# A fused recurrence and ELU feed-forward kernel on one core: a new order of vector work around three places, four closing additions on GpSimd, and the last two pairs' products interleaved

## The chip, the cores and the metric

One Trainium2 chip; the program runs on 1 of its cores. The metric is device time in microseconds (us), the median of several runs. Engines are named as in the profile: PE (TensorE, with PEld for its weight loads), DVE (VectorE), ACT (ScalarE), POOL (GpSimd), SP (SyncE, which issues most DMAs).

## The reference

```python
# q, k, v, f_logit: (4, 8, 768, 48) float32
f = 1.0 / (1.0 + np.exp(-f_logit))
for t in range(S):                       # S = 768
    state = f[:, :, t, :, None] * state + np.einsum('bhd,bhe->bhde', k[:, :, t], v[:, :, t])
    y[:, :, t] = np.einsum('bhd,bhde->bhe', q[:, :, t], state)
x = y.transpose(0, 2, 1, 3).reshape(3072, 384)
h = x @ w_in                             # w_in: (384, 2048)
g = np.where(h > 0.0, h, np.exp(np.minimum(h, 0.0)) - 1.0)
out = g @ w_out                          # w_out: (2048, 384)
```

## The kernel before, in words

The 3072 tokens are cut into 12 units of 256 tokens (`NU`), numbered 0 to 11, three to a batch. Each unit goes through the recurrence in chunked form ("attention") and then through the two matrix products of the feed-forward block. The hidden width 2048 is 16 blocks of 128, taken as 8 pairs per unit (index `P`, `m` the unit, `j` the pair). Everything is float32, and TensorE takes each float32 product in two passes, so a product counts as x2 in the profile.

**Up-products.** Units 0 and 1 compute `x @ w_in` directly (`up`, L980). From unit 2 on, `phase` (L954) computes four 128x128 blocks of hidden (a "quad", two pairs) with fewer products: a fast matrix scheme with 20 products of 128x128 per quad, in five phases of 3, 5, 5, 4 and 3 products. It uses precombined weights (`w_sums`, on DVE and POOL) and precombined inputs (`blend`, L938, six ops on POOL). Quad n has two PSUM banks, side 0 and side 1, under the tags h0 and h1; the side that quad n holds first is the tag that quad n+1 takes second. ACT copies the results of phases 0, 1 and 2 into the buffer `vals` (L968), and after phase 1 writes one of them back into the bank as the start of a sum (the "seed", L970), which phase 3 then adds to. DVE finishes the quad with `joins` (L946, L952): `JOIN3` and `JOIN4` read PSUM banks (3 and 2 instructions), `MID` and `LAST` read only `vals` (2 and 1 instructions). A bank is free for the next quad when the joins that read it are done.

**ELU.** `exped` (L972) runs two ACT instructions per pair, relu and exp, after `LAST`. `elu` (L993) runs one DVE instruction per pair (L996, tile `gg`), and then four POOL instructions (L1006, tile `sums`) that combine the four 128x128 blocks of `gg`.

**Down-products.** `down` (L1010) computes `g @ w_out` with seven products of 192 columns per pair (again a fast scheme), into four PSUM banks psM 0 to 3 of the unit (tags m0 to m3). Three products take `gg`, four take `sums`. After a unit's last pair (j = 7) its closing additions follow (L1061 to L1079): a copy of bank 0's first half to `u2`, then DVE additions that read the banks into the output tile `o`, and four stores on SP.

**Attention.** `attention` (L900) places per unit: `decays` (L696: a DVE scan, a DVE reciprocal, and POOL multiplications of k and q by the factors), three per unit, and `settle`; `transposed`; `both` (L891: `advance` on PE into psU under tags a0 and a1, `scores` on PE into the tags m3 and m0, `mask` on DVE, L773, and four state steps on DVE, L746); `outputs` (L794, PE, psY under tags a0 and a1 again); and `carried`.

**Order.** The order on each engine is the order in which the Python code issues it (a manual schedule). From unit 2 on, the loop at L1286 goes through 100 steps s; a step does two phases, the joins, the elus that are due, the attention work planned for this time (`at_step`, time T = 32 + 2s; a unit's time base is `base(u)`, 20 per unit), and some of the down-products from a running stream (`take`, which counts products). So each engine works its own queue in order, and waits at its head for what it needs. Steps 3 and 4 (131 to 139 us) hold three things at once: unit 1's last products and its closing additions, unit 2's second quad, and unit 3's `both`.

## Time and profile before

| what | value |
|---|---|
| median of 3 runs | 549.93 us (549.87, 549.93, 552.82) |
| the profiled execution: its own time | 551.41 us |
| its span, first to last instruction | 549.7 us |
| mean granted TensorE clock | 0.996 |
| PE busy | 531.6 us (97%) |
| DVE, ACT, POOL busy | 406.0, 313.6, 330.3 us |

A row of a timeline reads: start in us, length in us, engine, line, operation, output<-inputs, shape, count, and in brackets the engine's idle time ahead of it with what ended it. A row with x2 or more holds several instructions that followed each other. Matmuls are pipelined, so a PE row's length reaches beyond the start of the next one; start times are the better measure.

### The profile page before, as it was taken

The page shows a single profiled execution, that of the slowest core. Times are in us where ns is not written, and L with a number is a line of the kernel's source. Part 1 is how long each engine was busy: PE and PEld are TensorE (multiplying, and loading weights), DVE is VectorE, ACT ScalarE, POOL GpSimd, SP SyncE. Part 2 cuts the span into 40 slices and gives each one's busy share as a digit, 9 for nine tenths or more (in the row PEclk, how much of TensorE's full clock was granted, in tenths as well). Part 3 has the DMA queues.
Part 4 walks back from the last instruction along what each step waited for, and adds up shares of the span by engine and source line. Part 5 has one row for each costly group of instructions (what it writes and reads, how often), then busy time and mean ns, then how long its engine had stood idle before and what let it go on. Part 6 is the DMA issues. An engine that isn't in the chain of part 4 may idle for free.

```text
span 549.7 us, 15601 instructions
## 1 busy us (share of the span) xinstructions
PE 531.6 (97%) x6294; PEld 494.1 (90%) x6294; DVE 406.0 (74%) x721; ACT 313.6 (57%) x643; POOL 330.3 (60%) x556
## 2 busy tenths in 40 slices
PE   7889999999999999999999999999999999999995
PEld 3477778899899999999999999999999999999995
DVE  8699978875889687687687777777767865645562
ACT  3279675136455467567566566575575565564531
POOL 6510337779398288388378478468468567455452
PEclk9899999999999999999999999999999999999999
DMA  8998981024052261152252252253253212210001
GB/s 207 248 275 218 294 191 44 2 46 101 30 131 72 61 180 51 60 155 77 60 154 79 60 147 85 60 139 93 60 126 106 60 24 87 60 39 1 29 2 36
DMA packets 39474, 54.29 MB, mean 99 GB/s; under 512 B 4032, under 2 KB 29216, under 8 KB 39392
## 3 DMA queue, kind: packets, MB, share of 16 engines
q1 hardware_dynamic: 38592, 52.61, 35.8%
q8 instruction: 51, 0.84, 0.6%
q10 hardware_dynamic: 800, 0.59, 0.5%
q14 instruction: 31, 0.25, 0.2%
HBM read 45.02 MB, written 4.72 MB: 90 GB/s over the span
## 4 chain that ended last, share of the span: by engine, by line
PE 81%; DVE 7%; DMA 4%; ACT 3%; issue 2%; POOL 1%; SPq 0%; ACTq 0%; DVEq 0%; POOLq 0%
PE psM L1057 33%; PE psH L962 30%; PE psH L986 5%; PE psM L1019 3%; DVE vals L952 3%; PE psY L803 2%; DMA f<-f 2%; PE psY L827 2%; PE psU_a L788 2%; PE psS L765 2%; DMA f<-in_f_logit_dram 1%; PE psT L725 1%; DVE f L687 1%; ACT area L631 1%; DVE o L1067 1%
## 5 line engine op out<-in xcount | busy, mean ns | idle before, releaser
L1006 POOL TENSOR_TENSOR sums<-gg 128x128 f32<-128x128 f32 x172 | 100.9, 606 | 139.5 <-DVE gg L996 133.3
L968 ACT COPY vals<-psH 128x512 f32<-128x512 f32 (+1 forms) x120 | 65.4, 545 | 125.3 <-PE psH L962 119.1
L962 PE MATMUL psH<-xt,wi 128*128 128x128 f32 x880 | 132.6, 276 | 0.4 <-DVE vals L952 0.3
L952 DVE TENSOR_TENSOR vals<-vals,psH 128x256 f32<-128x256 f32 (+1 forms) x160 | 61.7, 386 | 89.8 <-ACT vals L968 43.8
L962 PE MATMUL psH<-xt,area 128*128 128x128 f32 x720 | 118.4, 278 | 1.8 <-DVE vals L952 0.9
L962 PEld LDWEIGHTS psH<-xt,wi 128*128 128x128 f32 x880 | 115.7, 192 | 1.9 <-issue 0.6
L962 PEld LDWEIGHTS psH<-xt,area 128*128 128x128 f32 x720 | 101.0, 191 | 3.5 <-PE psS L765 1.0
L1057 PE MATMUL psM<-area,sums 128*128 128x192 f32 x516 | 103.4, 327 | 0.0
L1057 PEld LDWEIGHTS psM<-area,sums 128*128 128x128 f32 x516 | 85.9, 190 | 0.2
L1057 PE MATMUL psM<-wo,gg 128*128 128x192 f32 x376 | 76.2, 327 | 0.5 <-DVE gg L996 0.5
L996 DVE SCALAR_TENSOR_TENSOR gg<-gg,vals 128x512 f32<-128x512 f32 x80 | 65.2, 849 | 11.6 <-ACT gg L977 11.6
L687 DVE RECIPROCAL f<-f 128x256 f32<-128x256 f32 x36 | 62.8, 1748 | 1.1
L1057 PEld LDWEIGHTS psM<-wo,gg 128*128 128x128 f32 x376 | 61.4, 190 | 1.4 <-DVE gg L996 0.6
L977 ACT ACTIVATE gg<-gg 128x512 f32<-128x512 f32 x96 | 60.5, 630 | 3.1
L952 DVE TENSOR_TENSOR vals<-vals 128x256 f32<-128x256 f32 x120 | 60.6, 518 | 2.1
L976 ACT ACTIVATE gg<-vals 128x512 f32<-128x512 f32 x80 | 49.5, 618 | 17.3 <-DVE vals L952 17.3
L677 POOL TENSOR_TENSOR q<-q,f 128x256 f32<-128x256 f32 x48 | 43.6, 910 | 19.4 <-DMA f<-f 12.8
L677 POOL TENSOR_TENSOR k<-k,f 128x256 f32<-128x256 f32 x48 | 36.6, 764 | 29.4 <-DMA f<-in_f_logit_dram 13.2
L942 POOL TENSOR_TENSOR xt<-xt 128x256 f32<-128x256 f32 x57 | 45.3, 808 | 3.2 <-DVE xt L942 1.8
L986 PE MATMUL psH<-xt,wi 128*128 128x256 f32 x192 | 44.8, 383 | 2.2 <-DVE xt L884 1.7
L1006 POOL TENSOR_TENSOR sums<-gg,sums 128x128 f32<-128x128 f32 x86 | 40.8, 475 | 6.7
L986 PEld LDWEIGHTS psH<-xt,wi 128*128 128x128 f32 x192 | 35.7, 190 | 8.8 <-DVE xt L884 1.8
(110 smaller groups left out, 747.2 us busy)
## 6 DMA issues: line engine op xcount, KB each, us to landing
area<-in_moe_w_out_dram SPq DMA_DIRECT2D x8, 768.0 KB, 9.7
again<-in_moe_w_in_dram SPq DMA_DIRECT2D x16, 384.0 KB, 4.0
again<-in_moe_w_out_dram SPq DMA_DIRECT2D x16, 384.0 KB, 3.2
k<-in_k_dram SPq DMA_DIRECT2D x12, 384.0 KB, 4.1
q<-in_q_dram SPq DMA_DIRECT2D x12, 384.0 KB, 5.3
v<-in_v_dram SPq DMA_DIRECT2D x12, 384.0 KB, 5.7
area<-in_moe_w_in_dram SPq DMA_DIRECT2D x8, 576.0 KB, 8.6
out_dram<-o SPq DMA_DIRECT2D x42, 96.0 KB, 1.7
```

The source lines that it names most:

```text
L677: e.tensor_tensor(out=t[n][:, p], in0=t[n][:, p], in1=t["f"][:, p, "kq".index(n)], op=ALU.mult)
L687: nc.vector.reciprocal(f[:, p, 1], f[:, p, 0])
L942: e.tensor_tensor(out=pick(x, to), in0=pick(x, a), in1=pick(x, b), op=ALU.subtract)
L952: nc.vector.tensor_tensor(out=pick(v, to), in0=x, in1=y, op=op)
L962: nc.tensor.matmul(bank[:, slot], lhsT=w_block(q, w), rhs=xts[m][:, x], start=(i < 2 and t == 0), stop=True, skip_group_check=True,)
L968: nc.scalar.copy(v[:, at : at + size], bank[:, frm : frm + size])
L976: nc.scalar.activation(g[:], h, AF.Relu, scale=-1.0)
L977: nc.scalar.activation(g[:], g[:], AF.Exp, scale=-1.0)
L986: nc.tensor.matmul(ph[:, i], lhsT=wi[j][:, kt, i * 128 : (i + 1) * 128], rhs=xts[m][:, 2 * kt : 2 * kt + 2].rearrange("n t f -> n (t f)"), ...
L996: nc.vector.scalar_tensor_tensor(out=g[:], in0=g[:], scalar=-1.0, in1=phs.pop(P), op0=ALU.add, op1=ALU.max)
L1006: nc.gpsimd.tensor_tensor(out=s[:, i], in0=x, in1=y, op=op)
L1057: nc.tensor.matmul(pm[bank][:, half * DH : (half + 1) * DH], lhsT=x, rhs=y, start=first, stop=(j == NP - 1), skip_group_check=True,)
```

## The change

- In the step loop, the elus that are due now come ahead of `MID` and `LAST` in every step (before, only in the last unit's steps). In the last unit's steps, a `MID` whose phase 3 is the second of its step waits for the next step, and comes after that step's `JOIN4`.
- In step 4 alone, `MID` and `LAST` are issued from inside `both`, after the masks (`hooks`).
- The first quad's exps move from the end of step 2 to the end of step 3; all exps of a step are issued ahead of its products, which moves nothing else on ACT.
- Unit 1's closing: `u2` is copied by DVE and not ACT; DVE keeps three additions; ACT copies banks 1 and 2 to SBUF (two copies of 384 columns, L1082); the last four additions run on POOL from those copies (L1085, two of 384 and two of 192 columns), and the stores follow them, all at time 43.
- In the last unit the first pair (j = 0) takes its products in the plain order, banks 0 and 3 first; the last two pairs take the sum for bank 0 fourth, POOL computes that sum second, and the products of the two pairs are interleaved.
- `decays`: unit 4's first is 2 times later (offset -9 for -11), unit 5's first two are 4 and 6 later (-15 and -9 for -19 and -15).

```diff
-    D4 = (-11, -5, -1, 1)
-    D5 = (-19, -15, -5, 1)
+    D4 = (-9, -5, -1, 1)
+    D5 = (-15, -9, -5, 1)
+    D6 = (-19, -15, -5, 1)
...
         mask(u, scores(u, ("m3", "m0")))
+        while hooks:
+            hooks.pop(0)()
...
+            if m == NU - 1 and j >= NP - 2:
+                todo[1], todo[2] = todo[2], todo[1]
...
-            if j == plain:
+            if j == plain and m < NU - 1:
                 todo = todo[2:5] + todo[:2] + todo[5:]
-            if j == NP - 1:
+            if j >= NP - 1 - (m == NU - 1):
                 todo = todo[:3] + todo[5:6] + todo[3:5] + todo[6:]
...
-            (nc.vector.tensor_copy if m == NU - 1 else nc.scalar.copy)(u2[:], p[0][0])
+            (nc.vector.tensor_copy if plain or m == NU - 1 else nc.scalar.copy)(u2[:], p[0][0])
...
+                c = sb.tile([128, 2 * DM], I32, tag="bits", name="banks")[:].bitcast(FP32)
+                for i in range(2):
+                    nc.scalar.copy(c[:, i * DM : (i + 1) * DM], pm[1 + i][:])
+
+                def close():
+                    put = lambda to, x, y: nc.gpsimd.tensor_tensor(out=to, in0=x, in1=y, op=ALU.add)
+                    put(u43[:], c[:, 0:DM].rearrange("p (h f) -> p h f", h=2), both_u2)
+                    put(flat[:, 3 * DH :], c[:, 0:DH], flat[:, 3 * DH :])
+                    put(flat[:, 3 * DH :], c[:, DH:DM], flat[:, 3 * DH :])
+                    put(flat[:, DH : 3 * DH], c[:, DM:], u43[:].rearrange("p h f -> p (h f)"))
+                    store(nc.sync, nc.sync)
+
+                at_step(PLAIN_UP * NFT + 11, close)
...
+        a, b = down(NU * NP - 2), down(NU * NP - 1)
+        for g in (a, a, a, a, b, b, b, a, b, a, b, b, a, b):
+            next(g, None)
+            yield
...
+                if i == 3 and ending and at:
+                    late.append((n, MID))
+                else:
+                    done.append((n, MID if i == 3 else LAST))
+            if i == 4:
+                done, late = late + done, []
         for P in elus.pop(s, ()):
             elu(P)
+        if s == 4:
+            hooks.extend(lambda n=n, todo=todo: joins(n, todo) for n, todo in done)
+        for n, todo in done:
+            if s != 4:
+                joins(n, todo)
+            if todo is LAST:
+                exps[s + (n % 2 if n else 1)] = n
         for f in plan.pop(T + 1, ()):
             f()
-        take((4, 4, 3, 3)[s] if s < 4 else (CHUNKS if T < base(NU - 1) else ENDING)[s % 10])
         if s in exps:
             exp_quad(exps.pop(s), s)
+        take((4, 4, 3, 3)[s] if s < 4 else (CHUNKS if T < base(NU - 1) else ENDING)[s % 10])
```

What this moves, in three places. On DVE in steps 3 and 4, before (u2, u43 and o1 are tiles of unit 1's closing, psM1_0 to psM1_3 its banks, vals1 and psH2_1 the second quad, gg2_0 and gg2_1 the first quad's pairs):

```order
L996 SCALAR_TENSOR_TENSOR gg2_0_1317<-gg2_0_1317,vals0_128 128x512
L996 SCALAR_TENSOR_TENSOR gg2_1_1320<-gg2_1_1320,vals0_128 128x512
L1067 TENSOR_TENSOR o1_1354<-psM1_3_886,u2_1_1355 128x192
L1067 TENSOR_TENSOR u2_1_1355<-psM1_0_883,u2_1_1355 128x192
L1067 TENSOR_TENSOR o1_1354<-psM1_3_886,u2_1_1355 128x192
L1067 TENSOR_TENSOR u43_1_1356<-psM1_1_884,u2_1_1355 128x384
L1067 TENSOR_TENSOR o1_1354<-psM1_1_884,o1_1354 128x192 x2
L1067 TENSOR_TENSOR o1_1354<-psM1_2_885,u43_1_1356 128x384
L952 TENSOR_TENSOR vals1_129<-vals1_129,psH2_1_1_1324 128x2x128 x2
L952 TENSOR_TENSOR vals1_129<-psH2_1_1_1324,vals1_129 128x128
L952 TENSOR_TENSOR vals1_129<-vals1_129,psH2_1_0_1307 128x2x128
L952 TENSOR_TENSOR vals1_129<-vals1_129,psH2_1_0_1307 128x128
```

And on DVE there now:

```order
L1073 TENSOR_TENSOR o1_1342<-psM1_3_886,u2_1_1343 128x192
L955 TENSOR_TENSOR vals1_129<-vals1_129,psH2_1_1_1318 128x2x128 x2
L955 TENSOR_TENSOR vals1_129<-psH2_1_1_1318,vals1_129 128x128
L955 TENSOR_TENSOR vals1_129<-vals1_129,psH2_1_0_1307 128x2x128
L955 TENSOR_TENSOR vals1_129<-vals1_129,psH2_1_0_1307 128x128
L999 SCALAR_TENSOR_TENSOR gg2_0_1333<-gg2_0_1333,vals0_128 128x512
L999 SCALAR_TENSOR_TENSOR gg2_1_1336<-gg2_1_1336,vals0_128 128x512
L774 TENSOR_TENSOR at3_1411<-psS3_0_1412,twice_111 128x512
L774 TENSOR_TENSOR at3_1411<-psS3_1_1413,twice_111 128x512
L955 TENSOR_TENSOR vals1_129<-vals1_129 128x2x128
L955 TENSOR_TENSOR vals1_129<-vals1_129 128x256
L955 TENSOR_TENSOR vals1_129<-vals1_129 128x2x128
```

Ahead of this stand the `u2` copy and the three kept additions; the joins that read PSUM now come first, then the two elus, then the masks, and `MID` and `LAST` last; before, the masks came after `LAST`. In both, the state steps follow.

On ACT in steps 2 to 4, before (vals0 is the first quad's buffer, vals1 the second's, the copy into psH2_1_1 is the seed):

```order
L976 ACTIVATE gg2_0_1317<-vals0_128 128x512
L977 ACTIVATE gg2_0_1317<-gg2_0_1317 128x512
L976 ACTIVATE gg2_1_1320<-vals0_128 128x512
L977 ACTIVATE gg2_1_1320<-gg2_1_1320 128x512
L968 COPY vals1_129<-psH2_1_1_1324 128x512
L970 COPY psH2_1_1_1324<-vals1_129 128x128
L968 COPY vals1_129<-psH2_1_0_1307 128x512
L1068 COPY u2_1_1355<-psM1_0_883 128x192
```

And on ACT there now:

```order
L971 COPY vals1_129<-psH2_1_1_1318 128x512
L973 COPY psH2_1_1_1318<-vals1_129 128x128
L971 COPY vals1_129<-psH2_1_0_1307 128x512
L979 ACTIVATE gg2_0_1333<-vals0_128 128x512
L980 ACTIVATE gg2_0_1333<-gg2_0_1333 128x512
L979 ACTIVATE gg2_1_1336<-vals0_128 128x512
L980 ACTIVATE gg2_1_1336<-gg2_1_1336 128x512
L1082 COPY banks_1349<-psM1_1_884 128x384
L1082 COPY banks_1349<-psM1_2_885 128x384
```

The seed and the copies around it went ahead of the first quad's four exp instructions, and two bank copies stand where the `u2` copy stood.

On PE at the program's end, the last unit's last two pairs (gg11_6 and sums11_6 are the last but one, gg11_7 and sums11_7 the last), before:

```order
L1057 MATMUL psM11_1_5719<-area_134,sums11_6_5869 128x192 x2
L1057 MATMUL psM11_0_5718<-area_134,sums11_6_5869 128x192
L1057 MATMUL psM11_2_5720<-wo_133,sums11_6_5869 128x192
L1057 MATMUL psM11_0_5718<-wo_133,gg11_7_5865 128x192
L1057 MATMUL psM11_3_5721<-wo_133,gg11_7_5865 128x192
L1057 MATMUL psM11_2_5720<-area_134,gg11_7_5865 128x192
L1057 MATMUL psM11_0_5718<-area_134,sums11_7_5875 128x192
L1057 MATMUL psM11_1_5719<-area_134,sums11_7_5875 128x192 x2
L1057 MATMUL psM11_2_5720<-wo_133,sums11_7_5875 128x192
```

And on PE there now:

```order
L1063 MATMUL psM11_0_5721<-area_134,sums11_6_5872 128x192
L1063 MATMUL psM11_0_5721<-wo_133,gg11_7_5868 128x192
L1063 MATMUL psM11_3_5724<-wo_133,gg11_7_5868 128x192
L1063 MATMUL psM11_2_5723<-area_134,gg11_7_5868 128x192
L1063 MATMUL psM11_1_5722<-area_134,sums11_6_5872 128x192
L1063 MATMUL psM11_0_5721<-area_134,sums11_7_5878 128x192
L1063 MATMUL psM11_1_5722<-area_134,sums11_6_5872 128x192
L1063 MATMUL psM11_1_5722<-area_134,sums11_7_5878 128x192 x2
L1063 MATMUL psM11_2_5723<-wo_133,sums11_6_5872 128x192
L1063 MATMUL psM11_2_5723<-wo_133,sums11_7_5878 128x192
```

Bank 0's last product is now the ninth of the fourteen and not the eleventh, bank 1's the twelfth and not the thirteenth; bank 2's stays the last.

35 lines of the change are left out of this document (13 added, 22 removed).

## The prediction

> **What bounds the kernel now.** I read the page's busy times first, then the windows (busy time of each engine in a stretch: length, PE, PEld, DVE, ACT, POOL), then the timeline wherever PE stands idle.
>
> ```profile
> PE 531.6 (97%) x6294; PEld 494.1 (90%) x6294; DVE 406.0 (74%) x721; ACT 313.6 (57%) x643; POOL 330.3 (60%) x556
> ```
> ```profile
> 229.00:504.00 275.00, 275.00 (x3468) 269.81 (x3467) 194.58 (x367) 172.69 (x398) 176.20 (x295) 1.00 0.30 84
> ```
> ```profile
> 204.61 1.78 PE psH L962 x16
> ...
> 533.15 9.48 PE psM L1057 x58
> ```
>
> PE bounds it. From 229 to 504 us it has no idle time at all, so nothing that DVE, ACT or POOL do earlier there can show in the time. The change adds and removes no product. It can only win PE's waits, and the tail after the last product. The last two rows, of the chain of waits, give the yardsticks: 16 passes of 128 columns in 1.78 us, 0.11 us each, and 58 passes of 192 columns in 9.48 us, 0.163 us each, 0.327 us a product. I price a wait as PE's start less the start that its products alone would have given.
>
> **Part A: steps 2 to 4, unit 1's end.**
>
> ```profile
> 132.09 0.63 ACT L976 ACTIVATE gg<-vals 128x512 f32<-128x512 f32 x1 [1.15 <-DVE vals L952]
> ...
> 134.20 0.49 PE L1057 MATMUL psM<-wo,sums 128*128 128x192 f32 x2
> ...
> 135.06 0.27 ACT L970 COPY psH<-vals 128x128 f32<-128x128 f32 x1
> ...
> 135.38 0.49 PE L962 MATMUL psH<-xt,area 128*128 128x128 f32 x2 [0.70 <-ACT psH L970]
> ...
> 138.11 1.12 PE L765 MATMUL psS<-q,k 64*64 64x64 f32 x64
> ...
> 138.81 0.87 DVE L952 TENSOR_TENSOR vals<-vals,psH 128x256 f32<-128x256 f32 x2
> ...
> 140.11 0.74 DVE L952 TENSOR_TENSOR vals<-vals,psH 128x256 f32<-128x256 f32 x2
> ...
> 140.15 0.91 PE L962 MATMUL psH<-xt,area 128*128 128x128 f32 x6 [0.91 <-DVE vals L952]
> 140.77 1.21 DVE L952 TENSOR_TENSOR vals<-vals 128x256 f32<-128x256 f32 x3
> ...
> 143.10 1.13 DVE L746 TENSOR_TENSOR state<-psU_a,state 128x192 f32<-128x192 f32 x3
> ...
> 144.41 1.16 PE L803 MATMUL psY<-at,v 64*64 64x64 f32 x64
> ```
>
> PE waits twice. The seed (135.06) stands on ACT behind four exp instructions that begin at 132.09; PE's natural start after 134.20 is 134.20 + 2 x 0.163 = 134.53, it starts at 135.38, so 0.85 us goes. Then `JOIN3` starts on DVE only at 138.81, after elus and all closing additions, and PE waits 0.91 for the bank (140.15).
>
> With the change the seed is ahead of the exps, and waits only for phase 1's products, long done: the first wait goes, and what took its place on ACT (four exps, two bank copies) is needed later. PE runs 0.85 earlier through the scores, which end at 138.11 + 1.12 - 0.85 = 138.38. They write banks 3 and 0 of the old unit, which DVE's `u2` copy and three additions have released long before: DVE is free from 132. `JOIN3` can start when phase 3's four products are out, about 134.53 + 8 x 0.11 + 0.2 = 135.6, and both joins take 140.85 - 138.81 = 2.04, to 137.65. That is before 138.38, so the second wait goes too.
>
> A new wait comes. `outputs` writes the banks a0 and a1 that the state steps read, and on DVE the elus now stand ahead of masks, `MID`, `LAST` and states. Rows for their lengths, with GpSimd idle and busy:
>
> ```profile
> 149.79 1.29 DVE L996 SCALAR_TENSOR_TENSOR gg<-gg,vals 128x512 f32<-128x512 f32 x2
> ...
> 161.11 1.82 DVE L952 TENSOR_TENSOR vals<-vals 128x256 f32<-128x256 f32 x3
> ...
> 170.98 1.81 DVE L996 SCALAR_TENSOR_TENSOR gg<-gg,vals 128x512 f32<-128x512 f32 x2
> ```
> ```profile
> L773 DVE TENSOR_TENSOR at<-psS,twice x24: 679/682/692, 23.9 to 478.2; 128x512 f32<-128x512 f32 x24
> ```
>
> The sums on POOL begin after the first elu and run for 4 us, so I take the first elu free and the second slowed: 0.65 + 0.9 = 1.55, to 139.2. Two masks 1.3 (they never vary), to 140.5. `MID` and `LAST` 1.82, since the sums run beside them (1.21 if they didn't), to 142.3. States 1.13, to 143.45, and PE follows at about 143.55. PE alone would be there at 138.38 + 16 x 0.11 + 12 x 0.163 + 0.1 = 142.2, so it now waits 1.3. Part A brings 144.41 - 143.55 = **0.86**; bounds 1.5 with the lengths of an idle GpSimd (1.21 and 0.65 for 1.82 and 0.9), and -0.24 where the second elu and the three `vals` instructions each lose a whole sum (0.475, below) and not 0.2 to 0.25: 4 x 0.275 = 1.1 more. I take the contended rows, as the sums are certain to be there.
>
> The four POOL additions must not delay what is queued behind them:
>
> ```profile
> 145.36 0.73 POOL L677 TENSOR_TENSOR k<-k,f 128x256 f32<-128x256 f32 x1 [4.78 <-DVE f L682]
> ...
> 150.62 1.18 POOL L1006 TENSOR_TENSOR sums<-gg 128x128 f32<-128x128 f32 x2 [4.54 <-DVE gg L996]
> ...
> 156.88 4.16 POOL L942 TENSOR_TENSOR xt<-xt 128x256 f32<-128x256 f32 x5
> ...
> 161.17 0.83 PE L962 MATMUL psH<-xt,area 128*128 128x128 f32 x6
> ```
> ```profile
> L1006 POOL TENSOR_TENSOR sums<-gg,sums 128x128 f32<-128x128 f32 x86 | 40.8, 475 | 6.7
> ```
>
> 128 columns take 0.475, 256 take 4.16 / 5 = 0.83, so 384 about 1.19 and 192 about 0.65: 2 x 1.19 + 2 x 0.65 = 3.7 us. They follow the k multiplication (145.36 + 0.73 - 0.86 = 145.25) and end at 148.95. The next sums could start at 150.62 - 0.86, less 0.87 as two `vals` joins no longer precede their elu: 148.9. So they fill a hole of 4.54 us almost exactly and cost nothing. Without that hole they would push sums, factors and the five blends, which end at 161.04, 0.13 ahead of the product that uses them (161.17). The stores that wait for them on SP hold up the next DMAs of x's gap rows and of later inputs by a microsecond or two; the blends that use x come 6 us later.
>
> **Part B: elus ahead of MID, and a decay moved away.**
>
> ```profile
> 166.75 1.75 DVE L687 RECIPROCAL f<-f 128x256 f32<-128x256 f32 x1
> ...
> 170.96 0.83 PE L962 MATMUL psH<-xt,area 128*128 128x128 f32 x6
> ...
> 172.25 0.92 PE L1057 MATMUL psM<-wo,gg 128*128 128x192 f32 x4 [0.45 <-DVE gg L996]
> ...
> 174.58 0.30 PEld L1057 LDWEIGHTS psM<-wo,sums 128*128 128x128 f32 x2 [0.30 <-POOL sums L1006]
> ...
> 183.74 0.63 PEld L962 LDWEIGHTS psH<-xt,area 128*128 128x128 f32 x5 [0.34 <-issue]
> ```
>
> The elus here (170.98) stand behind `MID` and, further up, behind the reciprocal of unit 5's first decay. PE's natural start is 170.96 + 6 x 0.11 = 171.62, so 0.62 is lost. Both go ahead of the elus no more: gg comes at least 1.5 us sooner, and **0.62** goes; of the 0.30 at 174.58 I count half, **0.15**, since PE itself shows no idle there. Unit 5's decays land at times 57, where one stood before, and 63, where DVE idles 3.13 us ahead of a join; a scan and a reciprocal take 0.94 + 1.75 = 2.7.
>
> ```profile
> 191.14 0.87 DVE L952 TENSOR_TENSOR vals<-vals,psH 128x256 f32<-128x256 f32 x2 [3.13 <-PE psH L962]
> ...
> 196.22 0.94 DVE L682 TENSOR_TENSOR_SCAN f<-f 128x256 f32<-128x256 f32 x1
> ```
>
> The 0.34 at 183.74 names no releaser; I count nothing for it, and keep it for the range.
>
> In all other units the same reorder meets a PE without idle time: nothing.
>
> **Part C: unit 11's first pair.**
>
> ```profile
> 514.40 0.82 DVE L1067 TENSOR_TENSOR o<-psM,u 128x192 f32<-128x192 f32 x2
> 514.43 0.61 PE L962 MATMUL psH<-xt,wi 128*128 128x128 f32 x4
> ...
> 515.28 0.59 PE L1057 MATMUL psM<-area,gg 128*128 128x192 f32 x2 [0.25 <-DVE o L1067]
> ```
>
> The first product goes to bank 2, which the closing reads last (to 515.22). Natural start 514.43 + 4 x 0.11 = 514.87: **0.41** lost. Now banks 0 and 3 come first, read long before, and bank 2 two products later, at 515.52: the wait goes.
>
> **Part D: MID after JOIN4.**
>
> ```profile
> 525.11 1.27 DVE L952 TENSOR_TENSOR vals<-vals 128x256 f32<-128x256 f32 x2
> ...
> 526.05 0.81 PE L1057 MATMUL psM<-area,sums 128*128 128x192 f32 x4
> ...
> 527.18 0.68 PE L962 MATMUL psH<-xt,wi 128*128 128x128 f32 x4 [0.32 <-DVE vals L952]
> ```
>
> `JOIN4` stands behind `MID`'s 1.27. Natural start 526.05 + 4 x 0.163 = 526.70: **0.48** lost. `JOIN4` will end near 525.9. `LAST` ends about where it did.
>
> **Part E: the tail.**
>
> ```profile
> 540.63 0.86 POOL L1006 TENSOR_TENSOR sums<-gg 128x128 f32<-128x128 f32 x2
> ...
> 542.13 1.14 PE L1057 MATMUL psM<-area,sums 128*128 128x192 f32 x6
> 542.66 0.36 DVE L1068 COPY u<-psM 128x192 f32<-128x192 f32 x1 [3.25 <-PE psM L1057]
> ```
>
> The `u2` copy starts 0.2 after bank 0's last product (542.13 + 0.33), and from there DVE works without a hole to the last store. That product comes two places earlier, 0.65; but its sum, now second on POOL, is ready at 540.63 + 0.43 + 0.475 = 541.54, signal included 541.6, against a start at 541.48: 0.12 waits. **0.53**.
>
> **Sum.** 0.86 + 0.62 + 0.15 + 0.41 + 0.48 + 0.53 = 3.05 us. The profiled execution ran 551.41 with a span of 549.7, so 548.4 and 546.6 for it; it lies 1.48 above the median of 549.93, and the same waits are in both, so I forecast 549.93 - 3.05 = **546.9**, 0.55% faster. A measurement tells about 0.5% here, 2.75 us, or 547.2.
>
> **Rivals.** *Better*: GpSimd slows DVE less, part A brings 1.5: 546.2.
>
> *DVE becomes the bound at the outputs.* If those four instructions lose 0.2 each beyond the rows, the states end near 144.3 and part A nets 0: 2.2 us, 547.7, within the bound. For it speaks that the sums of two pairs now run beside all four; against it, that the rows of a busy GpSimd show 0.2 to 0.25 each. The Trainium skill ("SBUF — State Buffer", "Who interferes with whom") says that a DVE instruction with two SBUF inputs and a GpSimd instruction that reads SBUF exclude each other, the second blocking fully, and that one with a single SBUF input is free; by full blocking part A is at its lower bound. The trace agrees on the masks (0.68 in all 24), and shows less than a full block on `vals`.
>
> *The closing tail doesn't move* since the copy waits for more than bank 0: part E 0, 547.4, within the bound. Against it: the 0.2 after bank 0's last product.
>
> *Slower: POOL becomes the bound in unit 3's stage.* The additions push sums, factors and blends, and PE waits at 161.17 for the blends. The chain has 1.7 - 0.86 + 0.13 = 1.0 us to spare, so beyond 4.7 us for the four additions each microsecond is lost; beyond 10.5 it is slower by over 0.5%. At 1.6 times my estimate (5.9) 1.2 would be lost: 548.1. At three times (11.1), 6.4: 553.3. No POOL row is slowed that far.
>
> **Chances.** The forecast 0.55, of which 0.42 beyond the bound and 0.13 within it, since it lies only 0.3 us beyond; better 0.15; DVE the bound 0.18; tail unmoved 0.06; slower 0.06. Faster 0.57, same 0.37, slower 0.06. Range: at the low end all waits go, 0.85 + 0.91 + 0.62 + 0.30 + 0.41 + 0.48 + 0.65, and the 0.34 at 183.74: 4.56, 545.4. At the high end A costs 0.24 and D and E bring nothing: 0.62 + 0.15 + 0.41 - 0.24 = 0.94: 549.0.
>
> **What would show it.** Right: no PE wait on the seed and none on the second quad's joins; the outputs of unit 3 waiting for states; POOL's four additions inside the hole; PE at unit 11's first product and at the last quad's second phase without idle time; the `u2` copy half a microsecond sooner against the last product. Wrong: PE idle ahead of the blends' first use, or a wait of one microsecond or more at a place that had none before, other than unit 3's outputs.

## The result, and the profile after

| | before | after |
|---|---|---|
| median, us | 552.04 (549.87 to 553.40, 11 runs) | 546.37 (545.73 to 548.94, 11 runs) |
| profiled execution, its span | 551.41, 549.7 | 546.03, 544.3 |

The ratio of the times is 0.9914, 95% interval 0.9897 to 0.9931: faster by 0.9%, 3.8 to 5.7 us. The forecast was 546.9, from a time of 549.93 before; in this series the kernel before took 552.04, so the time agrees better than the gain does (3.05 us forecast). A second series, in another session, gave 547.28 (12 runs) and a ratio of 0.9933 (0.9910 to 0.9956).

The page of the changed kernel answers with the same picture: PE nearly always busy, GpSimd busier by 8 us.

```profile
PE 528.5 (97%) x6294; PEld 492.8 (91%) x6294; DVE 407.5 (75%) x718; ACT 314.5 (58%) x644; POOL 338.4 (62%) x560
```

To see where the time went I start with a table by stages. A stage is the time between the starts of PE's passes at the same two places in its order in both traces (the same products, but for the last mark, where the order of the products is new), or from the last mark to the end of the span. In the changed kernel the marks are at 71.00, 132.53, 144.22, 178.87, 481.07 and 537.16 us. Up to 71 us PE waits for loads of weights and inputs, and that part scatters between runs of kernels that are the same there (70.8 to 73.1); it says nothing on the change. From 71 to 132.5 all kernels of this study take 61.52 to 61.56.

| stage | before | after | change | forecast |
|---|---|---|---|---|
| A: unit 1's end, to 144.22 | 13.34 | 11.69 | -1.65 | -0.86 |
| B: to unit 4's start, 178.9 | 36.25 | 34.65 | -1.60 | -0.77 |
| the middle, units 4 to 10 | 300.76 | 302.21 | **+1.45** | 0 |
| C and D: unit 11 | 56.93 | 56.08 | -0.85 | -0.89 |
| E: the tail | 8.03 | 7.15 | -0.88 | -0.53 |
| sum, with the 61.52 from 71 to 132.5 | 476.83 | 473.30 | -3.53 | -3.05 |

The sum is near the forecast, but two stages brought twice what they should, and the middle, costed at nothing, took 1.45 back.

**Stage A**, rows of the timeline after:

```profile
131.41 0.27 ACT L973 COPY psH<-vals 128x128 f32<-128x128 f32 x1
...
132.69 0.38 PE L965 MATMUL psH<-xt,area 128*128 128x128 f32 x2
...
135.82 1.29 DVE L999 SCALAR_TENSOR_TENSOR gg<-gg,vals 128x512 f32<-128x512 f32 x2
136.37 0.94 PE L965 MATMUL psH<-xt,area 128*128 128x128 f32 x6
136.58 1.25 POOL L1012 TENSOR_TENSOR sums<-gg 128x128 f32<-128x128 f32 x2 [2.04 <-DVE gg L999]
137.02 1.28 DVE L774 TENSOR_TENSOR at<-psS,twice 128x512 f32<-128x512 f32 x2
...
138.22 1.61 DVE L955 TENSOR_TENSOR vals<-vals 128x256 f32<-128x256 f32 x3
...
139.75 1.13 DVE L747 TENSOR_TENSOR state<-psU_a,state 128x192 f32<-128x192 f32 x3
...
140.63 1.46 PE L804 MATMUL psY<-at,v 64*64 64x64 f32 x64 [0.26 <-ACT gg L979]
...
142.73 1.00 POOL L1085 TENSOR_TENSOR u<-banks,u 128x384 f32<-128x384 f32 x1
...
143.68 1.26 POOL L1085 TENSOR_TENSOR o<-banks,o 128x192 f32<-128x192 f32 x2
...
144.90 1.01 POOL L1085 TENSOR_TENSOR o<-banks,u 128x384 f32<-128x384 f32 x1
...
146.60 1.37 POOL L1012 TENSOR_TENSOR sums<-gg 128x128 f32<-128x128 f32 x2 [0.69 <-DVE gg L999]
```

The seed is written at 131.41, a microsecond ahead of its product (132.69), and the product at 136.37 waits for nothing: the two old waits are gone. The new one is there, at unit 3's outputs (140.63), but small: 0.33, and 0.22 more inside the x64 row, against 1.3 forecast. (The row names an exp on ACT. The state steps are what it waited for: the second ends at 139.75 + 2/3 x 1.13 = 140.50, and a run below takes the wait away by moving them.) The four GpSimd additions run for 3.18 us, from 142.73 to 145.91, and GpSimd still idles 0.69 before the next sums: the hole held them.

**Stages B, C, D and E**, rows of the timeline after:

```profile
165.16 1.81 DVE L999 SCALAR_TENSOR_TENSOR gg<-gg,vals 128x512 f32<-128x512 f32 x2
...
168.04 0.82 PE L1063 MATMUL psM<-wo,gg 128*128 128x192 f32 x4
...
511.23 0.82 PE L1063 MATMUL psM<-wo,gg 128*128 128x192 f32 x4
...
522.78 0.61 PE L965 MATMUL psH<-xt,wi 128*128 128x128 f32 x4
...
537.52 0.36 DVE L1074 COPY u<-psM 128x192 f32<-128x192 f32 x1 [2.84 <-PE psM L1063]
...
538.29 0.81 PE L1063 MATMUL psM<-wo,sums 128*128 128x192 f32 x4
```

The elus of stage B begin 2.88 us ahead of their products (1.27 before). No row of unit 11 has a wait any more. The `u2` copy starts 1.58 us ahead of the last product's end (539.10), where it was 0.94.

**The middle.** Here the busy share of PE, on which I had relied, hides the loss. Weight loads, grouped by line, from 230 to 500 us; the last columns are the idle time ahead of them and who ended it. Before:

```profile
L962 PEld LDWEIGHTS psH<-xt,wi 128*128 128x128 f32 x572 | 75.3, 192 | 0.6 <-POOL xt L942 0.2
L1057 PEld LDWEIGHTS psM<-wo,gg 128*128 128x128 f32 x208 | 33.9, 190 | 0.1
```

After:

```profile
L965 PEld LDWEIGHTS psH<-xt,wi 128*128 128x128 f32 x572 | 74.9, 192 | 0.1
L1063 PEld LDWEIGHTS psM<-wo,gg 128*128 128x128 f32 x212 | 34.3, 190 | 1.2 <-DVE at L774 1.2
```

One wait went and another came. Before, the fast scheme's products waited in five of six units for GpSimd's last blend of x (the row puts 0.2 of the 0.6 down to it). After, the first products into a bank that the scores had used wait for the masks (L774 reads the scores there), 0.19 to 0.20 us in each of six units. In the six units between 226.7 and 477.8 the stretch from one unit's outputs to the next unit's end took 206.37 us before and 205.38 after, in five of them 0.18 to 0.23 less; the unit ends (some 7.4 us each, from the joins' banks to the outputs) took 44.16 before and 45.77 after.

### The profile page after: what moved, and what is told of

The parts are those of the page before. It is cut to its first block, busy times and chain, and to the rows that moved or that the text cites. A ratio compares the mean times of both kernels' runs of the same rounds, so it can differ in the third digit from the quotient of the medians.

```text
span 544.3 us, 15606 instructions
## 1 busy us (share of the span) xinstructions
PE 528.5 (97%) x6294; PEld 492.8 (91%) x6294; DVE 407.5 (75%) x718; ACT 314.5 (58%) x644; POOL 338.4 (62%) x560
## 4 chain that ended last, share of the span: by engine, by line
PE 89%; DMA 6%; DVE 2%; POOL 1%; issue 0%; ACT 0%; SPq 0%; ACTq 0%; DVEq 0%; POOLq 0%
PE psM L1063 37%; PE psH L965 33%; PE psH L989 6%; DMA area<-in_moe_w_in_dram 4%; PE psM L1025 3%; PE psY L804 2%; PE psY L828 2%; PE psU_a L789 2%; PE psS L766 2%; PE psT L726 1%; DMA f<-f 1%; DMA k<-in_k_dram 1%; DVE vals L955 1%; POOL k L678 0%; DVE gg L999 0%
## 5 line engine op out<-in xcount | busy, mean ns | idle before, releaser
L965 PEld LDWEIGHTS psH<-xt,wi 128*128 128x128 f32 x880 | 115.2, 192 | 0.7 <-DVE gg L999 0.3
L999 DVE SCALAR_TENSOR_TENSOR gg<-gg,vals 128x512 f32<-128x512 f32 x80 | 64.1, 837 | 9.4 <-ACT gg L980 9.4
L955 DVE TENSOR_TENSOR vals<-vals 128x256 f32<-128x256 f32 x120 | 64.2, 549 | 2.0
L678 POOL TENSOR_TENSOR q<-q,f 128x256 f32<-128x256 f32 x48 | 39.6, 826 | 18.8 <-DMA f<-f 14.6
L945 POOL TENSOR_TENSOR xt<-xt 128x256 f32<-128x256 f32 x57 | 48.6, 868 | 3.2 <-DVE xt L945 1.8
L1012 POOL TENSOR_TENSOR sums<-sums,gg 128x128 f32<-128x128 f32 x86 | 47.5, 552 | 0.2
```

Of the source, the lines that this page charges most:

```text
L678: e.tensor_tensor(out=t[n][:, p], in0=t[n][:, p], in1=t["f"][:, p, "kq".index(n)], op=ALU.mult)
L945: e.tensor_tensor(out=pick(x, to), in0=pick(x, a), in1=pick(x, b), op=ALU.subtract)
L955: nc.vector.tensor_tensor(out=pick(v, to), in0=x, in1=y, op=op)
L965: nc.tensor.matmul(bank[:, slot], lhsT=w_block(q, w), rhs=xts[m][:, x], start=(i < 2 and t == 0), stop=True, skip_group_check=True,)
L999: nc.vector.scalar_tensor_tensor(out=g[:], in0=g[:], scalar=-1.0, in1=phs.pop(P), op0=ALU.add, op1=ALU.max)
L1012: nc.gpsimd.tensor_tensor(out=s[:, i], in0=x, in1=y, op=op)
```

## Experiments

All kernels but the last are the changed kernel with the edit shown. The table repeats the stages; "from 71" leaves the loads out. The expectations speak of the stretch from unit 0's first output product (523.4 before, 519.9 after), which still holds some waits on loads of weights up to 73 us, so the verdicts go by the stages, which the expectations did not name. The stretch itself read 523.8 with part A undone, 520.8 decays, 519.1 order, 520.1 end, 519.0 exps early, 519.5 additions on DVE, 519.5 states first and 517.8 copy on DVE; all of these lie outside both ranges that were expected.

| kernel | A | B | middle | C, D | E | from 71 | ratio to before (95%) |
|---|---|---|---|---|---|---|---|
| before | 13.34 | 36.25 | 300.76 | 56.93 | 8.03 | 476.83 | |
| after | 11.69 | 34.65 | 302.21 | 56.08 | 7.15 | 473.30 | 0.9914 (0.9897 to 0.9931) |
| after, again | 11.70 | 34.64 | 302.72 | 56.08 | 7.19 | 473.86 | 0.9933 (0.9910 to 0.9956) |
| part A undone | 13.34 | 34.64 | 302.57 | 56.28 | 7.02 | 475.38 | 0.9952 (0.9928 to 0.9975) |
| decays undone | 11.69 | 35.81 | 302.59 | 56.09 | 6.75 | 474.46 | 0.9943 (0.9920 to 0.9967) |
| order undone | 11.69 | 35.22 | 301.03 | 56.07 | 7.03 | 472.59 | 0.9914 (0.9886 to 0.9942) |
| end undone | 11.69 | 34.64 | 301.31 | 56.88 | 7.40 | 473.45 | 0.9952 (0.9932 to 0.9972) |
| exps early | 12.04 | 34.63 | 301.13 | 56.07 | 6.78 | 472.19 | 0.9922 (0.9894 to 0.9951) |
| additions on DVE | 11.69 | 35.14 | 301.24 | 56.08 | 6.92 | 472.59 | 0.9913 (0.9885 to 0.9940) |
| states first | 11.70 | 34.63 | 301.43 | 56.07 | 6.80 | 472.16 | 0.9923 (0.9886 to 0.9961) |
| copy on DVE | 11.70 | 34.80 | **298.94** | 56.05 | 6.86 | 469.89 | 0.9859 (0.9810 to 0.9908) |
| copy on DVE, again | 11.69 | 34.63 | 300.22 | 56.05 | 6.91 | 471.07 | 0.9889 (0.9874 to 0.9905) |
| copy on DVE, old order | 11.69 | 35.10 | 300.26 | 56.05 | 6.93 | 471.57 | 0.9908 (0.9888 to 0.9927) |
| before, copy on DVE | 13.12 | 35.81 | 300.39 | 56.86 | 8.09 | 475.78 | 0.9992 (0.9975 to 1.0008) |

(The rows' stages leave out the 61.5 us from 71 to 132.5, which "from 71" holds.) Each stage is from one profile. How far one can be trusted shows in the kernels that don't touch it: A is 11.69 or 11.70 in all ten, B is 34.63 to 34.65 in seven of eight (34.80 in one), but the middle scatters: 301.1 to 302.7 in eight profiles with the new order and ACT's copy. Most of the timed ratios overlap the changed kernel's.

### One part undone at a time

**Part A**: the closing of unit 1 and the places of joins and exps in steps 0 to 4, as before.

```diff
-(nc.vector.tensor_copy if plain or m == NU - 1 else nc.scalar.copy)(u2[:], p[0][0])
+(nc.vector.tensor_copy if m == NU - 1 else nc.scalar.copy)(u2[:], p[0][0])
...
-                c = sb.tile([128, 2 * DM], I32, tag="bits", name="banks")[:].bitcast(FP32)
...
-                at_step(PLAIN_UP * NFT + 11, close)
+                add(u43[:], pm[1][:].rearrange("p (h f) -> p h f", h=2), both_u2)
+                add(flat[:, 3 * DH :], p[1][1], flat[:, 3 * DH :])
+                add(flat[:, 3 * DH :], p[1][0], flat[:, 3 * DH :])
+                add(flat[:, DH : 3 * DH], pm[2][:], u43[:].rearrange("p h f -> p (h f)"))
...
+        early = s < 5
+        for n, todo in done if early else ():
+            joins(n, todo)
...
-                exps[s + (n % 2 if n else 1)] = n
+                exps[s + n % 2] = n
```

> The changed kernel with part A taken back: unit 1's closing additions on DVE and its u2 copy on ACT as before, the first quad's exps at the end of step 2, and in steps 0 to 4 MID and LAST ahead of the elus and of the masks. All else stays changed. Measured from unit 0's first output product to the end, the profile of before has 523.4 us and the changed one 519.9. Theory 1 (each part earns its own waits, and keeps them): both waits of before at the seed (0.85) and at the second quad's joins (0.9) are back, the wait for the states at unit 3's outputs goes, and the stretch is 1.6 longer, 521.5. Rival (DVE and ACT pace the middle units, so that whatever PE wins early is partly given back there): the waits are back all the same, but by unit 10 the loss is under 1 us: 520.3 to 520.9.

Measured: stage A is back at 13.34 to the hundredth, 1.65 lost, and from 71 us on 2.08. That is the theory's size, and the rival (the middle levels it) falls: the middle was no better. The whole stretch read 523.8, because this run also met a wait of 1.04 at 72.6 on a late load of weights, which the edit doesn't touch.

**The decays' due times**, as before:

```diff
-    D4 = (-9, -5, -1, 1)
-    D5 = (-15, -9, -5, 1)
+    D4 = (-11, -5, -1, 1)
+    D5 = (-19, -15, -5, 1)
```

> The changed kernel with the three decays at their old times. Theory 1: unit 5's first decay stands ahead of the joins in unit 3's first steps again (2.4 us on DVE), but the elus go ahead of MID now, so of the wait for gg of 0.62 us half at most comes back: the stretch 519.9 to 520.2. Rival: the decay was the larger part of what part B won: 0.6 to 0.8 us back, 520.5 to 520.7.

Its timeline in stage B:

```profile
170.28 0.30 PEld L1063 LDWEIGHTS psM<-area,sums 128*128 128x128 f32 x2 [0.33 <-POOL sums L1012]
...
170.88 0.71 PEld L1063 LDWEIGHTS psM<-area,sums 128*128 128x128 f32 x4 [0.30 <-POOL sums L1012]
...
171.98 0.30 PEld L1063 LDWEIGHTS psM<-wo,sums 128*128 128x128 f32 x2 [0.40 <-POOL sums L1012]
```

Of stage B's 1.60, 1.16 is lost again: 1.0 as these waits for sums, 0.14 at the next quad's joins. GpSimd itself holds the sums up: they begin at 169.59, as its third multiplication of k and q by the decays' factors ends (166.63 to 169.63; the changed kernel has two there, 165.62 to 167.56), while the first elu had ended at 167.91. The wait for gg, which the theory had in mind, did not come back. Here the rival held, that the decay was the larger part, though it gave 0.6 to 0.8 and meant the wait for gg.

**The order** (the joins ahead of the elus again, from step 5 up to the last unit):

```diff
+        early = s > 4 and not ending
+        for n, todo in done if early else ():
+            joins(n, todo)
...
-            if s != 4:
+            if s != 4 and not early:
                 joins(n, todo)
```

> The changed kernel with MID and LAST ahead of the elus again in steps 5 to 90; part A, the decays and the end stay changed. Theory 1: only the wait for gg ahead of unit 3's down-products is open to it; with the decay moved away from there, DVE still reaches that elu about 1.4 us later (MID's two instructions), so 0 to 0.3 us of the 0.77 of part B comes back, and the other units show nothing: the stretch 519.9 to 520.3. Rival: the order of elus and MID pays in every unit (earlier sums on GpSimd): more than 0.1 us a unit, 1 us or more in all, 520.9 and up.

Stage B lost 0.57, more than the theory gave it and not where it looked: 0.40 for the blends near 163, 0.12 at the second quad's joins near 179.5, and nothing at the wait for gg. The stretch still came out at 519.1, since the middle took 1.18 less, where the rival had it lose 1 us or more; that is hardly clear of the middle's scatter (301.03 against 301.1 to 302.7). The timed ratio equals the changed kernel's, give or take 0.3%. So of the new order, the largest part of the diff by its reach, the timing shows no gain on balance; what it wins and loses in the middle is taken apart below.

**The end**: unit 11's product orders, the interleaving, the order of its sums and the late `MID`, as before.

```diff
-            if j == plain and m < NU - 1:
+            if j == plain:
...
-            if j >= NP - 1 - (m == NU - 1):
+            if j == NP - 1:
...
-        for P in range(PLAIN_UP * NP - LAG, NU * NP - 2):
+        for P in range(PLAIN_UP * NP - LAG, NU * NP):
...
-                if i == 3 and ending and at:
-                    late.append((n, MID))
-                else:
-                    done.append((n, MID if i == 3 else LAST))
+                done.append((n, MID if i == 3 else LAST))
```

> The changed kernel with the last unit as before: its first pair starts with bank 2, MID stays ahead of JOIN4, the last two pairs' products follow each other, and GpSimd's order of sums is the old one. Theory 1: waits of 0.41 (first pair, on DVE's last closing addition) and 0.48 (last quad, on JOIN4) are back, and the copy of bank 0 starts 0.65 later against the last product: 1.5 us, 521.4, as nothing behind them can level it. Rival: PE's lead at the last quad only moves the wait to the exps and sums of the last pairs, so that half of it or more is lost either way: 520.4 to 520.7.

Unit 11 is back at 56.88, within 0.05 of before, and the copy starts 0.94 us ahead of the last product's end again (538.31 against 539.25), where it was 1.58. From copy to the end of the span this run took 6.39, before 7.01 and after 6.78. DVE's share of that is 2.66 in all; the last store lands 2.48, 2.73 and 2.87 us behind DVE's last instruction, and the semaphore instructions that close the program take 1.25, 1.62 and 1.26 behind that. So the landing scatters by 0.4, which hides most of part E, and the closing instructions took 0.36 more before. The stretch (520.1) is lower than both expectations since the middle was 0.90 shorter than in the changed kernel's profile; the stages decide, and for the theory.

### Inside stage A

**Exps early**: unit 3's first four exps stand ahead of the seed on ACT again.

```diff
-                exps[s + (n % 2 if n else 1)] = n
+                exps[s + n % 2] = n
```

> The changed kernel with one thing put back: the four exp instructions of unit 3's first quad stand at the end of step 2 again, ahead of the seed copy on ACT. The stretch from unit 0's first output product to the end took 523.4 us before and 519.9 after. Theory (the seed's wait goes because the exps moved): PE waits 0.85 us again at the product that the seed starts (near 133), PE comes later to unit 3's outputs, so that the two waits there, 0.33 and 0.22, go in return: stretch 520.2 to 520.3. Rival (the exps' place doesn't matter, the bank copies stand in the same queue and were the cover): no wait at the seed, stretch 519.9.

```profile
133.52 0.27 ACT L973 COPY psH<-vals 128x128 f32<-128x128 f32 x1
...
133.84 0.49 PE L965 MATMUL psH<-xt,area 128*128 128x128 f32 x2 [0.70 <-ACT psH L973]
...
141.56 0.64 PE L804 MATMUL psY<-at,v 64*64 64x64 f32 x28
```

The seed's wait is back (0.87 by PE's starts) and the wait at the outputs is gone (no bracket at 141.56), so stage A loses 0.35: the theory, with its trade. Of A's 1.65 the exps' place is worth 0.35 in this kernel; the other 1.30 came with the closing additions' move and DVE's new order, which no run here takes apart.

**Additions on DVE**: the four deferred additions, at the same place.

```diff
-                    put = lambda to, x, y: nc.gpsimd.tensor_tensor(out=to, in0=x, in1=y, op=ALU.add)
+                    put = lambda to, x, y: nc.vector.tensor_tensor(out=to, in0=x, in1=y, op=ALU.add)
```

> The changed kernel with the four deferred closing additions on DVE instead of GpSimd, at the same place in the program. Theory (GpSimd carries what DVE has no room for): DVE idles only 0.70 us there and the four take about 1.7 (2 of 384 columns by 0.5, 2 of 192 by 0.35), so the next joins and elus come 1.0 later and PE waits 0.5 to 1.0 near 145 to 146: stretch 520.4 to 520.9. Rival (it was the deferral that paid, and the engine does not matter): no PE wait of over 0.2 near 145, stretch 519.9 to 520.1, and the masks and vals instructions of the stage run faster without GpSimd's additions beside them.

```profile
143.96 0.50 DVE L1085 TENSOR_TENSOR u<-banks,u 128x384 f32<-128x384 f32 x1
144.37 0.73 DVE L1085 TENSOR_TENSOR o<-banks,o 128x192 f32<-128x192 f32 x2
...
145.02 0.55 DVE L1085 TENSOR_TENSOR o<-banks,u 128x384 f32<-128x384 f32 x1
...
163.33 0.30 PEld L965 LDWEIGHTS psH<-xt,wi 128*128 128x128 f32 x2 [0.37 <-POOL xt L945]
```

The four take 1.6 us on DVE against 3.2 on GpSimd, and push the next elus back by 0.74 (from 145.52 to 146.60, less 0.34 of a later start), as foreseen; but PE doesn't wait at 145 to 146, and stage A is unchanged: the rival held, except that the two `vals` instructions behind the elus ran no faster (1.28, and 1.27 with GpSimd's additions ahead of them). The price comes 18 us later, at the blends, 0.34 at 163.33, most of the 0.49 that stage B loses. So stage A's gain doesn't need GpSimd for the additions; the engine is worth half a microsecond in stage B at most.

**States first**: unit 3's second and third joins behind its state steps.

```diff
-        while hooks:
-            hooks.pop(0)()
...
         for c in range(NC):
             step(u, c)
+        while hooks:
+            hooks.pop(0)()
```

> The changed kernel with unit 3's second and third joins moved from behind the masks to behind the state steps. Theory (the new wait at unit 3's outputs is the state steps behind those three instructions on DVE): the waits of 0.33 and 0.22 at the outputs go, nothing takes their place, since the exps that read the joined values come 1.1 later but are needed 3 us later: stretch 519.3 to 519.4. Rival (the wait moves on: the exps and with them the elus at 145.5 come later, and PE waits for gg or the sums near 146): stretch 519.9 or more.

```profile
141.88 1.16 PE L804 MATMUL psY<-at,v 64*64 64x64 f32 x64
...
145.41 0.34 ACT L811 COPY between<-psY 128x8 f32<-128x8 f32 x2
...
145.81 1.15 PE L828 MATMUL psY<-q,state 64*64 64x64 f32 x48 [0.56 <-ACT between L811]
```

The outputs wait no longer, so the state steps were what they waited for. But the joins now end 1.5 us later (against the same start), the four exps with them, and a small copy that stands behind those on ACT makes PE wait 0.63 at 145.81. Stage A is 11.70: the rival's result, by another wait than the one it named.

### The middle

What took 1.45 us back? After, DVE idles longer for ACT's copy `u2` at a unit's end. First the changed kernel's unit end, then the same one with the old order:

```profile
257.00 0.82 PE L1063 MATMUL psM<-wo,gg 128*128 128x192 f32 x4
...
258.87 0.32 ACT L1074 COPY u<-psM 128x192 f32<-128x192 f32 x1
...
259.22 0.36 DVE L1073 TENSOR_TENSOR o<-psM,u 128x192 f32<-128x192 f32 x1 [0.89 <-ACT u L1074]
...
264.57 1.28 DVE L774 TENSOR_TENSOR at<-psS,twice 128x512 f32<-128x512 f32 x2
...
265.90 0.62 PEld L1063 LDWEIGHTS psM<-wo,gg 128*128 128x128 f32 x4 [0.20 <-DVE at L774]
265.91 0.92 PE L1063 MATMUL psM<-wo,gg 128*128 128x192 f32 x4
```
```profile
257.32 0.82 PE L1063 MATMUL psM<-wo,gg 128*128 128x192 f32 x4
...
258.87 0.32 ACT L1074 COPY u<-psM 128x192 f32<-128x192 f32 x1
...
259.23 0.36 DVE L1073 TENSOR_TENSOR o<-psM,u 128x192 f32<-128x192 f32 x1 [0.48 <-ACT u L1074]
...
264.57 1.28 DVE L774 TENSOR_TENSOR at<-psS,twice 128x512 f32<-128x512 f32 x2
...
266.01 0.68 PEld L1063 LDWEIGHTS psM<-wo,gg 128*128 128x128 f32 x4
266.17 0.81 PE L1063 MATMUL psM<-wo,gg 128*128 128x192 f32 x4
```

By chance the two lie at the same times here, and can be read against each other. PE is 0.32 ahead with the new order (257.00 against 257.32). DVE is not: the additions start at 259.22 in both, because ACT's copy ends in both just ahead of that (258.87 + 0.32; DVE idles 0.89 in place of 0.48), and the masks at 264.57 in both. PE's lead doesn't reach the copy: in both kernels ACT works without a gap from the quad's first exp, which waits for DVE's joins (253.98 and 253.99), to the copy. So PE's lead ends in a wait for the masks: four products take 0.92, not 0.81, and the load ahead of them idles 0.20. The masks' chain is ACT's copy, five closing additions, joins, masks, with no hole after the copy. The test is to take the copy off ACT.

**The copy on DVE** in every unit:

```diff
-(nc.vector.tensor_copy if plain or m == NU - 1 else nc.scalar.copy)(u2[:], p[0][0])
+nc.vector.tensor_copy(u2[:], p[0][0])
```

> The changed kernel with the first closing copy on DVE in every unit, and not only in the units 1 and 11. After, DVE idles 0.89 us at a unit's end for ACT's copy, and PE waits 0.48 at 221 and 0.18 at 347 for the joins behind those additions. Theory (the middle units gave back up to 0.7 us of the lead because ACT's copy paces the unit's end): the copy takes 0.36 on DVE and starts at least 0.5 earlier, the waits go: stretch 519.2 to 519.4, with PE in no unit behind the changed kernel. Rival (these waits come and go from run to run, by 0.5 us, and DVE's queue sets the joins anyway): stretch 519.6 to 520.2.

The same unit end in that kernel, and its weight loads from 230 to 500 us:

```profile
256.98 0.82 PE L1063 MATMUL psM<-wo,gg 128*128 128x192 f32 x4
...
258.48 0.36 DVE L1074 COPY u<-psM 128x192 f32<-128x192 f32 x1 [0.17 <-PE psM L1063]
...
264.14 1.28 DVE L774 TENSOR_TENSOR at<-psS,twice 128x512 f32<-128x512 f32 x2
...
265.64 0.68 PEld L1063 LDWEIGHTS psM<-wo,gg 128*128 128x128 f32 x4
265.80 0.81 PE L1063 MATMUL psM<-wo,gg 128*128 128x192 f32 x4
```
```profile
L965 PEld LDWEIGHTS psH<-xt,wi 128*128 128x128 f32 x575 | 75.4, 192 | 0.0
...
L1063 PEld LDWEIGHTS psM<-wo,gg 128*128 128x128 f32 x212 | 34.6, 190 | 0.0
```

DVE idles 0.17 for the copy's product, the masks begin 0.43 earlier, and both waits of the middle are gone. The middle took 298.94: 3.27 less than after, more than the theory's 0.5 to 0.7, which counted only the two largest waits. Again, in more rounds (the expectations count the middle from 204.85, "its marks" below; the table's begins at 178.9):

> The kernel with every unit's first closing copy on DVE once more, in more rounds, beside the changed kernel on the same chip. The middle (units 4 to 10, the 276 us between the changed kernel's marks 204.85 and 481.0) took 275.02 us before, 276.23 after, and 273.49 with the copy on DVE. Theory (ACT's copy paces the unit's end): 273.4 to 273.7 again, no product into bank 3 waits for the masks, and a timed ratio to the kernel before of 0.983 to 0.988. Rival (one fortunate run): middle over 274.5, ratio 0.990 or more.

The middle read 300.22 here, 1.28 more than the first time and off the range (in its marks 274.73); 1.1 of that lies between 178.9 and 218.5, in waits the largest of which are 0.42 near 210 and 0.30 near 212. The unit ends are the same to the hundredth (43.88 us for the six), with no wait for masks; but unit 4's end, ahead of the six, has one again, 0.20 at 224.60. The middle is the rival's (over 274.5), and the ratio lies between the two. Timed: 544.64, ratio 0.9889; the changed kernel, in the same session, 547.28 and 0.9933. One edited line more makes this the fastest kernel of the study by its medians, but by less than its first trace promised.

**The changed kernel again:**

> The changed kernel itself, once more. Four kernels that equal it in the middle took 275.2 to 275.5 there and three took 276.2 to 276.8 (it took 276.23). Theory (the middle stands at the border of two limits, PE and the chain from ACT's copy over DVE to the masks, so it scatters by about 1 us from run to run): 275.2 to 276.5, with PE's weight loads waiting for the masks in all units. Rival (276.23 belongs to the changed kernel): 276.1 to 276.4, and waits of 0.48 and 0.18 at the joins of the same two units.

The middle took 302.72 (276.74 in the marks, above both ranges). The masks' wait is there as before (1.2 in the group's row); the larger waits are elsewhere: 0.51 in the unit at 347.8, where the first profile had 0.18, and 0.10 at 221, where that had 0.48 (and the kernels with part A and with the decays undone have 0.5). So these half-microsecond waits at a second quad's joins move from run to run, which speaks for the theory; its range was too narrow by 0.24. Why a run has them at one unit and not at another, I did not find out.

**Is it the order or the copy?** The copy on DVE with the old order (the two diffs "order" and "copy" together), and the kernel before with that copy alone:

```diff
-(nc.vector.tensor_copy if m == NU - 1 else nc.scalar.copy)(u2[:], p[0][0])
+nc.vector.tensor_copy(u2[:], p[0][0])
```

> The copy on DVE in every unit, and the joins ahead of the elus again from step 5 to the last unit. Theory (the new order does bring something in each middle unit, the blends' wait of 0.18 on GpSimd, and it could not be seen because ACT's copy took it back): these waits return, 7 to 8 of them, middle 274.6 to 275.0 against 273.49, and 0.5 more between 144 and 179. Rival (the order brings nothing in the middle, the copy alone does): middle 273.4 to 273.8.

> The kernel before with one edit: the first closing copy on DVE in every unit. Theory (before, the middle was bound by the blends, not by ACT's copy; the copy pays only once the elus come earlier): middle 274.6 to 275.0 against 275.02, and up to 0.4 at unit 1's end, where the joins stand behind the closing additions. Rival (the copy pays by itself): middle 273.4 to 273.8.

Over the same six units as above, stretches and unit ends come out so:

| | stretches | unit ends |
|---|---|---|
| before | 206.37 | 44.16 |
| order undone | 206.49 | 44.26 |
| before, copy on DVE | 206.36 | 43.89 |
| copy on DVE, old order | 206.38 | 43.88 |
| after | 205.38 | 45.77 |
| copy on DVE | 205.38 | 43.88 |

(Here "stretches" are from one unit's outputs to the next unit's end.) The two effects are separate. The new order takes 1.0 us out of the stretches, with or without the copy's move (the blends: PE's six products near 246 take 1.02 with the old order, 0.83 with the new). With ACT's copy it adds 1.6 to the unit ends (they are 45.3 to 46.4 in all eight profiles with both, so 1.0 to 2.3); with DVE's copy it adds nothing. And the copy alone, on the kernel before, brings 0.3 there, 0.22 in A and 0.44 in B by its profile, and a timed ratio of 0.9992 (0.9975 to 1.0008): nothing that the timing shows. By the middle as a whole both theories were close, 274.57 and 274.48 in the marks where they gave 274.6 to 275.0, and both rivals (273.4 to 273.8) fall; but with both edits the middle is 273.49 in one profile and 274.73 in the other, so it is the table of the six units, and not the whole, that separates the two effects.

## Why the prediction was right, and where it wasn't

- **What bounds the kernel.** Right in stages A, B, C, D and E, where PE's waits were read from its rows. Wrong in the step "From 229 to 504 us it has no idle time at all, so nothing that DVE, ACT or POOL do earlier there can show in the time", and so in "In all other units the same reorder meets a PE without idle time: nothing". A busy PE row can hold waits: a group of four products takes 0.92 and not 0.81, and by PE's starts 0.17 us goes at each unit's end. The trace of before had a sign, in PEld's row: idle 0.6, of which 0.2 for POOL's xt. The middle cost 1.45 (0.24 ahead of 204.85 and 1.21 behind it), made of -1.0 for the blends, +1.6 at the six unit ends, and +0.8 in and behind unit 4 (178.9 to 226.7), more than half of it one wait of 0.48 for joins near 221 that the second profile had elsewhere.
- **Part A**, 0.86 forecast, 1.65 measured; that is the rival "Better". Its bound of 1.5 was added up wrongly: with the lengths of an idle GpSimd it comes to 0.86 + 0.61 + 0.25 = 1.72. The joins' end was right to 0.01 us (forecast 137.65 in the time of before, less the 1.84 of the earlier start: 135.81; the elus began at 135.82). Each contended length that I added on top was too long: elus 1.20 from start to start and not 1.55, masks 1.20 and not 1.30, `vals` 1.53 and not 1.82, and the outputs start behind the second state step, not 0.1 behind the third: 0.35 + 0.10 + 0.29 + 0.35 = 1.09. The outputs' row gave 0.30 of that back: it took 1.46, with the wait for the third state step inside, and not 1.16. The sums began at 136.58, beside most of the second elu, and did not lengthen it. DVE as the bound at the outputs, the opposite rival, fell; so did the slower one: four additions in 3.18 us, 3.7 forecast, inside the hole.
- The Trainium skill ("SBUF — State Buffer", "Who interferes with whom") has DVE instructions with two SBUF inputs contend with GpSimd instructions that read SBUF, over a pair of ports that it calls an exclusive lock. The trace agrees that both suffer, and not that the second is stopped: three `vals` at 1.61 beside the sums, where 1.22 is usual, and sums at 0.62 where 0.45 is.
- **Part B**, 0.77 forecast, 1.60 measured. The named waits went. The decays undone cost 1.16 and the order undone 0.57, but neither brought the wait for gg (0.62) back: for that wait either edit is enough, and what each alone costs are other waits, for sums and for the blends, which I had at 0.15 and at nothing. I had given the gain to both edits at once without saying which. The 0.34 at 183.74, "issue" and without a releaser, for which I counted nothing, was real: 0.42 by PE's starts, gone after, and part of it (0.14) back with the decays undone. Another 0.1 were the blends, as in the middle.
- **Parts C and D**, 0.89 forecast, 0.85 measured, and back when undone (0.80).
- **Part E**: 0.53 forecast, the copy moved 0.64 against the last product; the feared wait on its sum (0.12) did not come, since GpSimd began these sums 0.36 earlier against PE (535.78, and 540.63 before, which is 536.14 in the time after). The other 0.24 lies behind DVE's last instruction: the stores landed 0.14 later there and the program's closing semaphore instructions took 0.36 less. That the change did this is not shown.
- **The sum.** 3.53 in the traces against 3.05, and 4.7 or 3.7 by the two timed ratios. Terms that were too small by 0.79, 0.83 and 0.35, and a loss of 1.45 that was not foreseen, nearly cancel. The number was right for partly wrong reasons.

What stays open: why the closing semaphore instructions took 1.62 and 1.60 us in the kernel before and in that kernel with its copy on DVE, and 1.20 to 1.28 in the twelve other profiles; why the unit-end waits of half a microsecond move between units from run to run, and with them 1 us of the middle; and the two medians of the changed kernel differ by 0.9 us between sessions.

## What to carry to other kernels

A stretch in which PE is busy from end to end can still hold waits, so read the weight loads' idle time and the mean length of a group of products, too, before an edit there is costed at nothing. When an edit makes PE faster between two of its waits, follow the other engines' chain to the next point where PE needs them: if that chain doesn't get faster as well, the gain is handed back there, and the next edit worth making is on that chain. Time by stages between the same two instructions tells such a gain and loss apart when the total can't.

## What was not expected of the hardware

- The two 384-column additions take 1.00 and 1.01 us on GpSimd and 0.50 and 0.55 on DVE, with all operands in SBUF; the copy of 192 columns out of PSUM takes 0.32 on ACT and 0.36 on DVE. An engine's place in the chain, not its speed, decided where the copy belongs.
- The last store landed 2.48 to 2.91 us after DVE's last instruction, over the fourteen profiles, with the same DVE instructions ahead of it: a scatter of 0.4 us, nearly what a whole part of this change (part E, 0.53) was to bring.
